# Score units one by one with the products in pieces between them, and an output or value step ahead of the gate step

## The chip, the cores and the metric

One core of a Trainium2 chip (trn2) runs the whole program. The metric is the device time of one execution in microseconds; each kernel was run several times, and medians are given with lowest and highest. The profile's span is about 1.8 us shorter than the time of the same run (461.3 of 463.1). A run is called slow when it is over 1.5% above the fastest of its kernel; such runs are left out of medians and ratios. A run also carries the mean clock that TensorE was granted. That number matters here: in the runs with a trace, 0.995 or 0.996 goes with one stretch of 3.4 us at half clock, 0.999 or 1.00 with none before the last few us.

## The reference

Softmax attention for 8 sequences, 12 heads, 448 tokens, head dimension 64; then a gated feed-forward block on the 3584 x 768 result.

```python
scores = q @ k.transpose(0, 1, 3, 2) / sqrt(64)          # (8, 12, 448, 448)
attn = softmax(scores) @ v                               # (8, 12, 448, 64)
x = attn.transpose(0, 2, 1, 3).reshape(3584, 768)
g = x @ w_gate                                           # (3584, 1536)
out = (g * sigmoid(g) * (x @ w_val)) @ w_out             # (3584, 768)
```

## The kernel before

Work is cut into *pairs* of heads (48), a pair into four *score units* of one key chunk (112 keys): two matmuls of 448 columns into a score buffer, and one exponential of 896 columns on ScalarE. There are three score buffers, and transposed q and k and the gate groups use the same three.

```python
def qk(pr, c):                                    # a score unit
    s = ps_s.tile([128, 2, 512], FP32, tag="s")   # ps_s has 3 buffers
    ...                                           # two matmuls
    nc.scalar.activation(e[:, :, 0:S], s[0:P, :, 0:S], AF.Exp, scale=sm_scale)

def pv(pr):                                       # the product of a pair: 4 x 8 matmuls of 65 columns
    acc = ps_f.tile([128, 512], FP32, tag="f", name="acc")   # ps_f has 2 buffers
    for c in range(NC):
        ...
    nc.vector.reciprocal(...)                     # then one multiply for 6 blocks, two small ones
    ...
```

`copy_v` puts V of a pair beside a column of ones (which gives the sums of the softmax); `turn_x` transposes a pair's result with TensorE into the feed-forward input X. The first six pairs come before any feed-forward work, because X of the first sequence needs all six. That *first batch* is the stage of part 1 of the change:

```python
for pr in range(FIRST):                           # FIRST = 6
    qk_half(pr, 0, ...)                           # two score units
    ...
    if pr in (2, 4):
        for p in range(3):
            copy_v(3 * (pr // 2 - 1) + p)         # VectorE
    elif pr == 3:
        pv(1)                                     # a whole product at once
        turn_x(0)
    ...
    qk_half(pr, 1, turn2)
    if pr == 2:
        pv(0)
    elif pr == 3:
        turn_x(1)
        pv(2)
    ...
```

After that come *visits*: three score units (two in the first four visits), the products of pairs that are due, and some feed-forward steps. A feed-forward step of the first kind (`run_fv`) is a gate group and a value group of 6 matmuls each; of the second kind (`run_o`) an output step of 12 matmuls.

```python
def ffn1_steps(kk, c0, n, hts):
    for fb in range(NFB):
        gp = ps_s.tile([128, 2, 512], FP32, tag="s", name="gp")[:, 0]   # a score buffer
        ...                                       # 6 matmuls
        nc.scalar.activation(sg[:, 0:n], gp[:, 0:n], AF.Tanh, scale=0.5)
        vp = ps_f.tile([128, 512], FP32, tag="f")
        ...                                       # 6 matmuls
        nc.vector.scalar_tensor_tensor(t1[:, 0:n], sg[:, 0:n], 1.0, gp[:, 0:n], ALU.add, ALU.mult)
        nc.vector.scalar_tensor_tensor(hts[:, fb, 0:n], t1[:, 0:n], 0.5 * HS, vp[:, 0:n], ALU.mult, ALU.mult)
```

In 17 visits no product is due. In 12 of these the gate group follows three score units directly and has to wait for a score buffer (below: *bare* visits). The other 5 have only one or two score units, or no gate group, and show no such wait; the flag `bare` in the code holds for all 17.

The softmax here doesn't subtract the row's maximum and nothing guards it: scores larger than these inputs give would overflow.

## Time and profile before

| | before |
|---|---|
| time, median of 3 runs | 463.11 us (463.1 to 464.29) |
| span of the profiled run, mean granted clock | 461.3 us, 0.996 |
| TensorE busy | 442.3 us, 96% |
| gate groups' waits for an exponential | 8.0 us, 12 times |
| first gate group starts at | 34.31 us |
| granted clock in the stretch 15.15 to 18.57 | 0.52 |

The page's first part and its chain of waits say what bounds the kernel; the prediction shows those lines. TensorE's timeline in the kernel before shows how a bare visit looks (start, duration, line, work, number of matmuls; in brackets the idle time just before it and what ended it):

```profile
92.96 0.35 PE L217 MATMUL s<-qkT 64*128 64x448 f16 x2
94.00 1.45 PE L297 MATMUL gp<-X,wg 128*128 128x512 f16 x6 [0.69 <-ACT E L225]
95.29 1.46 PE L309 MATMUL vp<-X,wv 128*128 128x512 f16 x6
```

The last score unit has gone in, and the gate group stands 0.69 us until the first of three exponentials has left its buffer.

### The profile page before, as it was taken

The numbers are of one execution on the slowest core, as the hardware profiler recorded it, in microseconds if no ns is written. First come the engines' busy times: TensorE is split into PE (matmuls) and PEld (weight loads), VectorE is DVE, ScalarE is ACT, GpSimd is POOL, SyncE is SP. The second block draws the span as 40 slices with busy tenths as digits, with TensorE's granted clock in tenths as the row PEclk, the third lists the DMA queues.
The fourth block names the chain that finished last, engine by engine and source line by source line (L and its number), as shares of the span: only waits on it lengthen the run. The fifth ranks groups of instructions, "written<-read, shape, count | busy, mean of one in ns | idle before, by whom it ended". The sixth has DMA issues, their size and how long they took to land.

```text
span 461.3 us, 9838 instructions
## 1 busy us (share of the span) xinstructions
PE 442.3 (96%) x3992; PEld 247.2 (54%) x3992; DVE 207.3 (45%) x480; ACT 237.7 (52%) x350; POOL 137.9 (30%) x222
## 2 busy tenths in 40 slices
PE   7879999999999999999999999999999999999996
PEld 3645566545455656455455565555455556644464
DVE  3576664456553534344344453444435343235400
ACT  6774577655565455635555455654554634222222
POOL 8455607834614225252322404350100000000000
PEclk9899999999999999999999999999999999999999
DMA  9999999999855648894567558973344111210033
GB/s 132 196 200 202 177 193 163 197 171 129 100 84 80 114 93 130 120 110 80 82 114 117 96 98 118 136 97 70 56 67 75 36 21 50 76 34 1 0 104 102
DMA packets 104941, 48.71 MB, mean 106 GB/s; under 512 B 59584, under 2 KB 101440, under 8 KB 104896
## 3 DMA queue, kind: packets, MB, share of 16 engines
q0 software_dynamic: 43296, 23.37, 40.7%
q1 hardware_dynamic: 61504, 24.66, 28.7%
q8 instruction: 31, 0.51, 0.5%
q14 instruction: 14, 0.11, 0.1%
q10 hardware_dynamic: 96, 0.05, 0.0%
HBM read 47.19 MB, written 11.01 MB: 126 GB/s over the span
## 4 chain that ended last, share of the span: by engine, by line
PE 93%; ACT 5%; DVE 1%; issue 0%; ACTq 0%
PE gp L297 24%; PE op L343 24%; PE vp L309 24%; PE acc L242 9%; PE s L217 8%; ACT E L225 4%; PE acc L251 3%; PE wp L107 1%; PE tp L205 1%; ACT osb L350 1%; PE xtp L283 0%; DVE xt L261 0%; DVE xt L268 0%; DVE qkT L191 0%; DVE R L260 0%
## 5 line engine op out<-in xcount | busy, mean ns | idle before, releaser
L225 ACT ACTIVATE E<-s 112x896 f16<-112x896 f32 x192 | 161.7, 920 | 23.1 <-PE s L217 22.9
L297 PE MATMUL gp<-X,wg 128*128 128x384 f16 (+1 forms) x576 | 124.8, 352 | 8.0 <-ACT E L225 8.0
L309 PE MATMUL vp<-X,wv 128*128 128x384 f16 (+1 forms) x576 | 124.6, 352 | 0.0
L343 PE MATMUL op<-wo,hts 128*128 128x384 f16 (+1 forms) x684 | 115.9, 323 | 0.0
L317 DVE SCALAR_TENSOR_TENSOR t<-sg,gp 128x384 f32<-128x384 f32 (+1 forms) x96 | 59.6, 621 | 107.0 <-ACT sg L305 107.0
L305 ACT ACTIVATE sg<-gp 128x384 f32<-128x384 f32 (+1 forms) x96 | 52.7, 549 | 77.5 <-PE gp L297 75.7
L343 PEld LDWEIGHTS <-hts 128*128 128x128 f16 x684 | 66.3, 98 | 44.1 <-issue 0.4
L350 ACT ACTIVATE osb<-op 128x384 f32<-128x384 f32 (+1 forms) x57 | 27.6, 485 | 116.0 <-PE op L343 113.3
L309 PEld LDWEIGHTS <-wv 128*128 128x128 f16 x576 | 56.4, 98 | 52.7
L297 PEld LDWEIGHTS <-wg 128*128 128x128 f16 x576 | 53.1, 97 | 55.6 <-issue 12.4
L165 POOL COPY qk<-q 112x512 f16<-112x512 f16 x37 | 22.9, 620 | 143.5 <-DMA qkT<-qk 142.4
L320 DVE SCALAR_TENSOR_TENSOR hts<-t,vp 128x384 f16<-128x384 f32 (+1 forms) x96 | 59.6, 621 | 10.4 <-DVE t L317 0.5
L242 PEld LDWEIGHTS <-E 112*128 112x128 f16 x1152 | 47.0, 98 | 16.4 <-issue 15.9
L242 PE MATMUL acc<-vo,E 112*128 112x65 f16 x1152 | 52.6, 195 | 0.3 <-DVE X L286 0.3
L217 PE MATMUL s<-qkT 64*128 64x448 f16 x384 | 50.3, 356 | 2.4 <-ACT E L225 1.6
L260 DVE RECIPROCAL R<-acc 128x7 f32<-128x7 f32 x48 | 9.9, 206 | 92.9 <-PE acc L251 92.8
L251 PE MATMUL acc<-vo,E 112*128 112x65 f16 x384 | 43.2, 194 | 0.0
L134 POOL DMA_DIRECT2D vraw<-in_v_dram x40 | 26.6, 666 | 24.0 <-DVE vo L140 9.9
L127 POOL DMA_DIRECT2D k<-in_k_dram x42 | 27.8, 661 | 12.6 <-PE vp L309 8.4
L217 PEld LDWEIGHTS <-qkT 64*128 64x128 f16 x384 | 14.4, 94 | 28.5 <-issue 20.9
L127 POOL DMA_DIRECT2D q<-in_q_dram x42 | 28.0, 667 | 4.1 <-PE tp L205 2.3
L261 DVE TENSOR_TENSOR xt<-acc,R 128x384 f16<-128x384 f32 x48 | 26.8, 558 | 1.7
(38 smaller groups left out, 155.2 us busy)
## 6 DMA issues: line engine op xcount, KB each, us to landing
q<-in_q_dram POOLq DMA_DIRECT2D x37, 112.0 KB, 4.1
k<-in_k_dram POOLq DMA_DIRECT2D x37, 112.0 KB, 4.7
vraw<-in_v_dram POOLq DMA_DIRECT2D x36, 112.0 KB, 4.5
out_dram<-osb SPq DMA_DIRECT2D x7, 336.0 KB, 3.2
wg<-in_moe_w_gate_dram POOLq DMA_DIRECT2D x8, 288.0 KB, 10.9
wv<-in_moe_w_val_dram POOLq DMA_DIRECT2D x8, 288.0 KB, 11.3
wo<-in_moe_w_out_dram POOLq DMA_DIRECT2D x2, 1152.0 KB, 22.7
out_dram<-osb SPq DMA_DIRECT2D x8, 288.0 KB, 3.3
```

The source lines that it names most:

```text
L127: nc.gpsimd.dma_start(dst[:, ds(h0, 2 * n)], flat.rearrange("h (p c) d -> p h (c d)", c=NC))
L217: nc.tensor.matmul(s[:, hx, 0:S], lhsT=t[ts(hx, 64), c * P : c * P + 128], rhs=t[ts(hx, 64), ds(S + (1 - hx) * D, S)], start=True, stop=True,)
L225: nc.scalar.activation(e[:, :, 0:S], s[0:P, :, 0:S], AF.Exp, scale=sm_scale)
L242: nc.tensor.matmul(a7[:, 2 * j + hx], lhsT=e[:, ds(c * EB + 9 * hx + 2 * j, 2)].rearrange("p b x -> p (b x)"), rhs=vo[:, hx, c, 0 : D + 1] ...
L251: nc.tensor.matmul(a7[:, 6], lhsT=e[:, ds(b0, 2)].rearrange("p b x -> p (b x)"), rhs=vo[:, hx, c, 0 : D + 1], start=False, stop=last and h ...
L297: nc.tensor.matmul(gp[:, 0:n], lhsT=wslice("g", fb, cb), rhs=X[kk][:, cb, ds(c0, n)], start=(cb == 0), stop=(cb == NCB - 1),)
L305: nc.scalar.activation(sg[:, 0:n], gp[:, 0:n], AF.Tanh, scale=0.5)
L309: nc.tensor.matmul(vp[:, 0:n], lhsT=wslice("v", fb, cb), rhs=X[kk][:, cb, ds(c0, n)], start=(cb == 0), stop=(cb == NCB - 1),)
L317: nc.vector.scalar_tensor_tensor(t1[:, 0:n], sg[:, 0:n], 1.0, gp[:, 0:n], ALU.add, ALU.mult)
L320: nc.vector.scalar_tensor_tensor(hts[:, fb, 0:n], t1[:, 0:n], 0.5 * HS, vp[:, 0:n], ALU.mult, ALU.mult)
L343: nc.tensor.matmul(op[:, 0:w], lhsT=hts[:, fb, ts(ch, 128)], rhs=wo[oh][:, fb, ds(m0 - oh * OH, w)], start=(fb == 0), stop=(fb == NFB - 1),)
L350: nc.scalar.activation(osb[:, ds(m0, w)], op[:, 0:w], AF.Copy, scale=1.0 / HS)
```

## The change

Part 1 wants the exponentials of the first batch to run without gaps: score units go in one at a time, and from unit 12 up to two *pieces* of a product (8 matmuls, one key chunk) follow each. Single warming matmuls are to keep the clock up, and the first six copies of V move to GpSimd. Part 2 wants the bare visits' wait away: an output step goes first, or, where there is none, the value group before the gate group.

```diff
-NV = 3
+NV = 6
     def copy_v(pr):
-        nc.vector.tensor_copy(Vts[pr % NV][:, :, :, 0:D], vraw[:, pr % VS])
+        eng = nc.gpsimd if pr < FIRST else nc.vector
+        eng.tensor_copy(Vts[pr % NV][:, :, :, 0:D], vraw[:, pr % VS])
@@ the product is cut into pv_chunk(pr, c); turn_x uses 5 matmuls for 4, and in the first batch the product's own accumulator; for 12 pairs one multiply of 448 columns for three @@
@@ the first batch @@
+        for u in range(FIRST * NC):
+            pr, c = divmod(u, NC)
+            qk(pr, c)
 ...
+            elif u >= 6 and c == 2:
+                prep(pr + 2)()
+            if u in (5, 7, 8, 9, 11):
+                dummy(1)
+            if c == 1:
+                if pr in (1, 3):
+                    for p in range(3):
+                        copy_v(3 * (pr // 2) + p)
+                for w in wq.pop(pr, []):
+                    emit(w)
+            if u in (15, 17, 19, 21):
+                turn_x((u - 15) // 2)
+            for _ in range(2):
+                if u >= 12 and pieces[0][0] * NC + pieces[0][1] <= u - 3:
+                    piece()
@@ ffn1_steps @@
+            if val_first[0]:
+                val_first[0] = False
+                vp = ps_f.tile([128, 512], FP32, tag="f", name="vp")
+                group("v", vp)
             gp = ps_s.tile([128, 2, 512], FP32, tag="s", name="gp")[:, 0]
+            group("g", gp)
@@ a visit of the first two sequences' blocks, and of the later ones @@
+            bare = not todo and bool(chunks)
             if adds[max(y for y in adds if y <= x)] < 2:
+                if bare and oq and not fvq:
+                    carry -= run_o()
+                elif bare:
+                    val_first[0] = True
                 carry = run_budget(left() / (end - x) + carry)
             else:
 ...
+                if bare and no:
+                    run_o()
+                    no -= 1
+                elif bare:
+                    val_first[0] = True
```

More of the change, by code (lines that the diff above doesn't have):

```diff
@@ L193, in turn0 @@
                 if t == 0:
-                    nc.vector.tensor_copy(qkT[pr][:, 2 * S :], tp[:, 0, 0:D])
+                    tq = tp
+            nc.vector.tensor_copy(qkT[pr][:, 2 * S :], tq[:, 0, 0:D])
         def turn():
@@ L231, in qk_half, with pv_chunk @@
                 between()
-    def pv(pr):
+    accs = {}
+    def pv_chunk(pr, c):
+        if c == 0:
+            accs[pr] = ps_f.tile([128, 512], FP32, tag="f", name="acc")
         e = Es[pr % NE]
         vo = Vts[pr % NV]
-        acc = ps_f.tile([128, 512], FP32, tag="f", name="acc")
-        a7 = acc[:, 0 : 7 * (D + 1)].rearrange("p (s d) -> p s d", s=7)
-        for c in range(NC):
-            first, last = c == 0, c == NC - 1
-            for j in range(3):
-                for hx in range(2):
-                    nc.tensor.matmul(
-                        a7[:, 2 * j + hx],
-                        lhsT=e[:, ds(c * EB + 9 * hx + 2 * j, 2)].rearrange("p b x -> p (b x)"),
-                        rhs=vo[:, hx, c, 0 : D + 1],
-                        start=first and j + hx == 0,
-                        stop=False,
-                    )
+        a7 = accs[pr][:, 0 : 7 * (D + 1)].rearrange("p (s d) -> p s d", s=7)
+        for j in range(3):
@@ L249, in pv @@
             for hx in range(2):
-                b0 = c * EB + 6 + hx
                 nc.tensor.matmul(
-                    a7[:, 6],
-                    lhsT=e[:, ds(b0, 2)].rearrange("p b x -> p (b x)"),
+                    a7[:, 2 * j + hx],
+                    lhsT=e[:, ds(c * EB + 9 * hx + 2 * j, 2)].rearrange("p b x -> p (b x)"),
                     rhs=vo[:, hx, c, 0 : D + 1],
-                    start=False,
-                    stop=last and hx == 1,
-                )
+                    start=c + j + hx == 0,
@@ L258, in pv @@
+                    stop=False,
+                )
+        for hx in range(2):
+            nc.tensor.matmul(
+                a7[:, 6],
+                lhsT=e[:, ds(c * EB + 6 + hx, 2)].rearrange("p b x -> p (b x)"),
+                rhs=vo[:, hx, c, 0 : D + 1],
+                start=False,
+                stop=c == NC - 1 and hx == 1,
+            )
+        if c < NC - 1:
+            return
         r = attp.tile([128, 8], FP32, tag="R", bufs=2, name="R")
         xt = Xts[pr % NX]
+        n = 7 if pr < XPE else 6
@@ L260, in pv @@
         nc.vector.reciprocal(r[:, 0:7], a7[:, :, D])
         nc.vector.tensor_tensor(
-            xt[:, 0:3].rearrange("p j (h d) -> p (j h) d", h=2),
-            a7[:, 0:6, 0:D],
-            r[:, 0:6].unsqueeze(2).to_broadcast([128, 6, D]),
+            xt[:].rearrange("p j (h d) -> p (j h) d", h=2)[:, 0:n],
+            a7[:, 0:n, 0:D],
+            r[:, 0:n].unsqueeze(2).to_broadcast([128, n, D]),
             ALU.mult,
         )
+        if pr < XPE:
+            return
         for hx in range(2):
@@ L270, in pv @@
             )
+    def pv(pr):
+        for c in range(NC):
+            pv_chunk(pr, c)
     def turn_x(pr):
@@ L279, in turn_x @@
         if pr < XPE:
-            tp = ps_f.tile([128, 512], FP32, tag="f", name="xtp")
-            for j in range(4):
-                n = 128 if j < 3 else D
+            tp = accs[pr] if pr < FIRST else ps_f.tile([128, 512], FP32, tag="f", name="xtp")
+            for j in range(3):
                 nc.tensor.matmul(
-                    tp[:, ds(D + 128 * j if j < 3 else 0, n)], lhsT=xt[:, j], rhs=ident[:, 0:n], start=True, stop=True
+                    tp[:, ds(D + 128 * j, 128)], lhsT=xt[:, j], rhs=ident[:], start=True, stop=True
+                )
+            for hx in range(2):
+                nc.tensor.matmul(
+                    tp[ts(hx, D), 0:D],
+                    lhsT=xt[:, 3, 0:D],
+                    rhs=ident[:, ts(hx, D)],
+                    start=True,
+                    stop=True,
                 )
@@ L291, in turn_x, with group @@
         nc.sync.dma_start_transpose(dst[:, 0:D].rearrange("p (j q) -> p j q", j=1), xt[0:D, 3])
+    val_first = [False]
     def ffn1_steps(kk, c0, n, hts):
         for fb in range(NFB):
-            gp = ps_s.tile([128, 2, 512], FP32, tag="s", name="gp")[:, 0]
-            for cb in range(NCB):
-                nc.tensor.matmul(
-                    gp[:, 0:n],
-                    lhsT=wslice("g", fb, cb),
-                    rhs=X[kk][:, cb, ds(c0, n)],
-                    start=(cb == 0),
-                    stop=(cb == NCB - 1),
-                )
+            gp = vp = None
+            def group(kind, dst):
+                for cb in range(NCB):
+                    nc.tensor.matmul(
+                        dst[:, 0:n],
+                        lhsT=wslice(kind, fb, cb),
+                        rhs=X[kk][:, cb, ds(c0, n)],
+                        start=(cb == 0),
+                        stop=(cb == NCB - 1),
+                    )
+            if val_first[0]:
+                val_first[0] = False
+                vp = ps_f.tile([128, 512], FP32, tag="f", name="vp")
+                group("v", vp)
+            gp = ps_s.tile([128, 2, 512], FP32, tag="s", name="gp")[:, 0]
+            group("g", gp)
             sg = fp.tile([128, 512], FP32, tag="sg")
             nc.scalar.activation(sg[:, 0:n], gp[:, 0:n], AF.Tanh, scale=0.5)
-            yield NCB * n / 2400.0
-            vp = ps_f.tile([128, 512], FP32, tag="f")
-            for cb in range(NCB):
-                nc.tensor.matmul(
-                    vp[:, 0:n],
-                    lhsT=wslice("v", fb, cb),
-                    rhs=X[kk][:, cb, ds(c0, n)],
-                    start=(cb == 0),
-                    stop=(cb == NCB - 1),
-                )
+            if vp is None:
+                vp = ps_f.tile([128, 512], FP32, tag="f", name="vp")
+                group("v", vp)
             t1 = fp.tile([128, 512], FP32, tag="t1")
@@ L322, in ffn1_steps @@
             )
-            yield NCB * n / 2400.0
+            yield
     def ffn2_steps(kk, c0, n, hts, first, last_block):
@@ L381 @@
             nc.vector.memset(e[:, 7::EB], 0.0)
-        for xt in Xts:
-            nc.vector.memset(xt[D:128, 3], 0.0)
         for vo in Vts:
@@ L431, in run_fv @@
             gen, t = fvq.pop(0)
-            for _ in range(2):
-                next(gen)
+            next(gen)
             return 2 * t
@@ L450, in share, with piece @@
             return (at + 1) * total // n - at * total // n
-        for pr in range(FIRST):
-            odd = pr % 2 == 1
-            turn2 = None
-            qk_half(pr, 0, prep(2) if pr == 1 else None)
-            if pr == 0:
+        pieces = [(p, c) for p in range(FIRST) for c in range(NC)]
+        def piece():
+            pv_chunk(*pieces.pop(0))
+        for u in range(FIRST * NC):
+            pr, c = divmod(u, NC)
+            qk(pr, c)
+            if u == 1:
                 dummy(1)
@@ L459 @@
                 dummy(1)
-            if pr > 0:
-                turn2 = prep(pr + 2)
-            if pr in (2, 4):
-                for p in range(3):
-                    copy_v(3 * (pr // 2 - 1) + p)
-            elif pr == 3:
-                pv(1)
-                turn_x(0)
-            elif pr == 5:
-                turn_x(3)
-            for w in wq.pop(pr, []):
-                emit(w)
-            qk_half(pr, 1, turn2)
-            if pr == 0:
-                dummy(2)
-            if pr == 2:
-                pv(0)
-            elif pr == 3:
-                turn_x(1)
-                pv(2)
-            elif pr == 4:
-                turn_x(2)
-                pv(3)
-            elif pr == 5:
-                pv(4)
+            elif u == 3:
+                dummy(2)
+            elif u == 4:
+                prep(2)()
+            elif u >= 6 and c == 2:
[13 more added lines that the diff above has]
+                    piece()
         queue = []
@@ L515 @@
             if x == 0:
+                piece()
                 turn_x(4)
-                pv(5)
+                piece()
+                piece()
                 turn_x(5)
```

## The prediction

> **What bounds the kernel now.** I read the page first, then the waits of TensorE, then the busy time in stretches, then the timelines of TensorE, VectorE, ScalarE and GpSimd up to the first feed-forward block, and last the order of the instructions of both kernels on each engine, which can be listed without a run.
>
> ```profile
> PE 442.3 (96%) x3992; PEld 247.2 (54%) x3992; DVE 207.3 (45%) x480; ACT 237.7 (52%) x350; POOL 137.9 (30%) x222
> PE 93%; ACT 5%; DVE 1%; issue 0%; ACTq 0%
> ```
>
> TensorE is busy for 96% of the span and the chain that ended last runs through it for 93%. Nothing in the change takes matmuls away worth counting, so all that can be won is TensorE's idle or slow time. The waits of TensorE:
>
> ```profile
> PE gp L297 <- ACT E L225: 8.0, 12, 0.7
> PE xtp L283 <- DVE xt L261: 1.7, 3, 0.9
> PE s L217 <- ACT E L225: 1.6, 5, 0.4
> PE tp L205 <- ACT E L225: 1.1, 2, 0.7
> PE s L217 <- DVE qkT L191: 0.6, 1, 0.6
> PE acc L242 <- DVE X L286: 0.3, 1, 0.3
> ```
>
> The first line is 12 gate groups that wait 0.67 us each for an exponential, all after 56 us. The other lines lie in the first 35 us. The stretches there (columns: length, busy time and count of PE, PEld, DVE, ACT, POOL, then granted clock, DMA share, GB/s):
>
> ```profile
> 8.33:11.74 3.41, 2.84 (x40) 1.32 (x39) 1.06 (x4) 3.29 (x5) 3.36 (x5) 1.00 1.17 139
> 11.74:15.15 3.41, 2.09 (x36) 1.24 (x31) 1.07 (x4) 3.41 (x6) 1.53 (x2) 1.00 1.41 189
> 15.15:18.57 3.42, 3.39 (x43) 2.26 (x43) 1.94 (x8) 2.11 (x3) 1.11 (x2) 0.52 1.43 198
> 18.57:21.98 3.41, 3.05 (x70) 2.34 (x68) 2.52 (x7) 2.93 (x4) 2.55 (x4) 0.98 1.32 203
> 21.98:25.39 3.41, 2.49 (x54) 1.75 (x51) 3.24 (x11) 2.22 (x3) 1.56 (x3) 1.00 1.36 198
> ```
>
> ScalarE fills 11.74 to 15.15 completely: 12 exponentials ran there in a row, 10.02 us from 6.72, so 0.835 us each. In the next stretch the clock is 0.52 and ScalarE starves behind two whole product blocks. The first gate matmul starts at 34.31. From 35 us on TensorE's only waits are those 12.
>
> **What the Trainium skill says.** "TensorE: Matmul & The Clock Gate", Part 1, says that a monitor halves the clock for a following window of about 3413 ns after a window with too little activity. The trace agrees: 2.09 us busy of 3.41 was followed by a window at 0.52, 2.49 of 3.41 was not. "PSUM — Partial Sum Buffer", section "Engine vs sequencer instructions", says that ScalarE, VectorE and GpSimd have strict first-in-first-out queues. The trace agrees for GpSimd: its issues wait one behind the other, as below. "SBUF — State Buffer", section "SBUF: two separate sides", says that VectorE (in some modes) and GpSimd hold a shared port for a whole instruction. GpSimd's query load begins at 15.35, after VectorE's copies of V that began at 14.80; that fits, but is one case.
>
> **The change, part 1: the first batch.** It takes the 24 score units one by one, puts up to two pieces of a product (8 matmuls, one key chunk) after each from unit 12, adds single warming matmuls after five units, and moves the six copies of V from VectorE to GpSimd, with six buffers for three. If ScalarE were the bound throughout, exponential 23 would end at 6.72 + 24 x 0.835 = 26.8. After it come: the last piece 0.24 and its drain 0.2, reciprocal 0.21, the multiply, now 448 wide, 0.56 x 448/384 = 0.65, the transposes 0.25, with hand-overs of 0.05: the first group would start near 28.5, against 34.31, 5.8 us sooner. TensorE's own work allows about that: per unit 0.27 for scores, 0.48 for two pieces, and 0.51 for a transposition of q and k every fourth: 10.8 us for units 12 to 23.
>
> But the copies stand in GpSimd's queue, and that is where I expect the loss:
>
> ```profile
> 15.35 0.74 POOL L127 DMA_DIRECT2D q<-in_q_dram  x1 [1.32 <-PE tp L205]
> 18.20 0.71 POOL L127 DMA_DIRECT2D k<-in_k_dram  x1 [2.10 <-PE s L217]
> 18.90 1.64 POOL L151 DMA_DIRECT2D wg<-in_moe_w_gate_dram  x2
> 21.27 0.76 POOL L151 DMA_DIRECT2D wv<-in_moe_w_val_dram  x1 [0.73 <-DMA wg<-in_moe_w_gate_dram]
> 22.71 0.76 POOL L151 DMA_DIRECT2D wv<-in_moe_w_val_dram  x1 [0.67 <-DMA wg<-in_moe_w_gate_dram]
> 24.44 0.74 POOL L127 DMA_DIRECT2D q<-in_q_dram  x1 [0.96 <-DMA wv<-in_moe_w_val_dram]
> ```
>
> The issues recycle eight semaphores, so each waits for an earlier transfer to land, while the DMA is full (198 GB/s). Copies 0 to 2 stand before the load at 15.35 and can run when V lands at 14.80; a GpSimd copy of that shape takes 0.62 (the copies of q and k), so the first is ready at 15.5, when unit 12 needs it. Copies 3 to 5 stand behind the value weight load at 22.71, which waits for gate weights to land. They end at 23.47 + 0.62 = 24.1, 24.7 and 25.3. Unit 18 wants the first of them: 15.2 + 7 x 0.27 + 12 x 0.24 + 2 x 0.51 + 2 x 0.25 = 21.5. So TensorE stands for 2.6 us, and ScalarE, with units up to 18 queued, runs dry at 22.6.
>
> From 24.15, by the order listed: unit 18's pieces 0.48; 19: 0.27 + 0.25 (a turn of x) + 0.48; 20: 0.75; 21: 0.76; 22: 0.27 + 0.51 + 0.24; 23: 0.51; then two scores, pieces 21 to 23 and a turn 1.5. Sum 6.0, end at 30.2; plus 1.5 for the chain above: 31.7. That is 2.6 us won instead of 5.8. If the stall also halves the clock in the window after 25.39 (chunks took 0.44 instead of 0.24 at 0.52), about 1.5 more is lost and 1.1 is won. Weighing the halved clock 0.45, the plain stall 0.35 and no stall (4.8) 0.2, I take 2.2.
>
> **Part 2: visits without products.** Three score units fill the three score buffers, so a gate group after them waits for the first exponential. In nine of the twelve visits an output step of 12 matmuls (1.95 us) now goes first. It needs another pool, whose buffer is long free, and outlasts the 0.67. Nothing else moves: all nine vanish, together 8.0 - (0.63 + 0.69 + 0.63) = 6.05 us.
>
> Four visits put the value group first. In three, and in one early one that had no wait, only one pair of groups is run, so the gate group is now the last thing before the next three scores. The third of those takes the gate group's buffer, which VectorE frees after ScalarE's tanh:
>
> ```profile
> L317 DVE SCALAR_TENSOR_TENSOR t<-sg,gp 128x512 f32<-128x512 f32 x48 | 33.0, 688 | 59.6 <-ACT sg L305 59.6
> L317 DVE SCALAR_TENSOR_TENSOR t<-sg,gp 128x384 f32<-128x384 f32 x48 | 26.6, 554 | 47.5 <-ACT sg L305 47.5
> L305 ACT ACTIVATE sg<-gp 128x512 f32<-128x512 f32 x48 | 28.7, 597 | 49.3 <-PE gp L297 47.6
> L305 ACT ACTIVATE sg<-gp 128x384 f32<-128x384 f32 x48 | 24.0, 500 | 28.2 <-PE gp L297 28.1
> ```
>
> For 512 columns: drain 0.17 + tanh 0.60 + 0.69 + hand-overs 0.13 = 1.59 after the gate group, while the third score is due at 0.1 + 0.48 = 0.58. So a wait of 1.0 replaces one of 0.66: two visits lose 0.4 each, 0.8. For 384 columns the chain is 1.35: the visit at 56.7 us keeps nearly all its loss (won 0.1), because tanh there is held by the three exponentials in both orders; the early visit gets a new wait of 0.75. Before, the value group lay in between and hid this. Six turns of x get a fifth matmul, 0.04 each: 0.2.
>
> Part 2: 6.05 + 0.1 - 0.8 - 0.75 - 0.2 = 4.4 us. VectorE's saving (one wider multiply for three instructions in twelve pairs) is off the path.
>
> **Sum.** 463.1 - 2.2 - 4.4 = 456.5 us, 1.4% faster.
>
> **Rivals.** (A) Everything works as intended: copies on time, no moved waits: 5.8 + 8.0 gives 449 to 450. For it: exponentials have run gaplessly for 12 units. Against it: the queue order above. (B) The waits only move, and the first batch stalls at half clock or worse: 1 + 2.5 gives 459.5 to 460. For it: the single buffer ring of three and the 0.52 stretch. Against it: nine of the twelve visits have the harmless output step. (C) Transfers become the bound as TensorE arrives earlier: the output weights land at about 64.5 and 72.1 (GpSimd's issues that wait for them start at 64.53 and 72.06), the first output group started at 71.8; moved to 68 it still has its half, and the second half is needed some 8 us later. Pair 14's transpose, issued at 73.9, takes 3 to 12 us, needed at 88.2 before. So perhaps a microsecond at most; I leave it out of the sum.
>
> **Range and chances.** First batch 0.5 to 5, part 2 3 to 6: 80% between 453.2 and 460.0. Over 2% needs less than 453.85, which asks that the stall be absent and part 2 whole: 0.17. Slower by 2%: 0.01. Within: 0.82.
>
> **What would show it.** A TensorE wait for GpSimd's copy of V ahead of the first product of pair 3, ending near 24.1; the first value group near 31.7; the granted clock in the window after it; no gate waits for exponentials; new score waits for VectorE's gate product, about 1.0 twice and 0.7 to 0.8 twice. I am wrong if copies 3 to 5 run before 21.5, if a copy takes much more than 0.62, or if output steps first produce waits of their own.

## The result, and the profile after

The changed kernel takes 456.77 us (456.47 to 456.91, 4 runs) beside 463.7 us (463.1 to 464.3, 4 runs) for the kernel before: a ratio of 0.985, 95% interval 0.9831 to 0.9868. A ratio here is the mean time of one kernel's fast runs over that of the other's of the same rounds, so not quite the ratio of the medians. That is 1.5% faster. All four of these runs of the kernel before lie at 463.1 us or above, where its later runs with a halved clock lie (see The experiments); beside its runs without (461.8) the changed kernel is 5.0 us faster, 1.1%.

The page of the changed kernel, its busy line and its chain of waits:

```profile
PE 444.9 (98%) x4009; PEld 247.9 (54%) x4009; DVE 200.2 (44%) x450; ACT 238.7 (52%) x350; POOL 141.7 (31%) x228
...
PE 94%; ACT 3%; DVE 2%; issue 0%; DVEq 0%
```

TensorE is busy for 2.6 us more in a span 6.2 us shorter. The waits of TensorE in the changed kernel (us in total, times, longest):

```profile
PE s L219 <- DVE t L339: 3.1, 4, 0.9
PE wp L107 <- DVE warm L401: 1.2, 1, 1.2
PE acc L293 <- DVE xt L266: 1.0, 1, 1.0
PE acc L245 <- DVE qkT L211: 0.8, 1, 0.8
PE s L219 <- ACT E L227: 0.2, 1, 0.2
```

The 12 gate waits of 8.0 us are gone. In their place four score units wait 3.1 us for VectorE's gate product. The fourth line is a new wait before a product, which I come to below. The stretches of the first batch in the changed kernel, with the columns of the prediction's table:

```profile
11.74:15.15 3.41, 3.05 (x29) 1.38 (x29) 1.18 (x3) 3.41 (x5) 1.53 (x2) 1.00 1.40 185
15.15:18.57 3.42, 3.27 (x64) 2.29 (x63) 1.14 (x5) 3.42 (x5) 3.11 (x6) 1.00 1.43 198
18.57:21.98 3.41, 3.41 (x68) 2.36 (x65) 2.12 (x6) 2.48 (x4) 2.28 (x3) 1.00 1.32 203
21.98:25.39 3.41, 2.65 (x58) 1.95 (x57) 2.06 (x5) 1.73 (x3) 2.75 (x5) 1.00 1.38 199
25.39:28.80 3.41, 3.41 (x72) 2.43 (x71) 2.04 (x4) 2.87 (x4) 2.64 (x4) 1.00 1.35 201
```

The granted clock stays at 1.00. ScalarE is full up to 18.57, and from there it is TensorE that is full (3.41 of 3.41) in two of three stretches, while ScalarE starves. The first feed-forward group, now a value group, starts at 32.89 against 34.31: 1.4 us of the 6.2 come from the first batch (against a run that had the halved stretch), 4.8 from the visits behind it.

The stall before pair 3's first product, on TensorE's timeline in the changed kernel:

```profile
22.43 0.36 PE L219 MATMUL s<-qkT 64*128 64x448 f16 x2
22.73 0.39 PE L207 MATMUL tp<-ident,q 112*64 112x112 f16 x8
22.95 0.36 PE L207 MATMUL tp<-ident,k 112*64 112x112 f16 x8
24.07 0.34 PE L245 MATMUL acc<-vo,E 112*128 112x65 f16 x6 [0.76 <-DVE qkT L211]
```

And GpSimd's timeline there, in the same kernel:

```profile
15.42 1.72 POOL L141 COPY vo<-vraw 112x512 f16<-112x512 f16 x3 [0.79 <-DMA vraw<-in_v_dram]
...
21.18 0.77 POOL L152 DMA_DIRECT2D wv<-in_moe_w_val_dram  x1 [0.69 <-DMA wg<-in_moe_w_gate_dram]
22.64 0.76 POOL L152 DMA_DIRECT2D wv<-in_moe_w_val_dram  x1 [0.69 <-DMA wg<-in_moe_w_gate_dram]
23.39 1.72 POOL L141 COPY vo<-vraw 112x512 f16<-112x512 f16 x3
```

The first of three copies starts at 23.39 and takes about 0.6 us, so it ends near 24.0, just before the product starts at 24.07. The profile names VectorE as the releaser of that wait, but the product doesn't read what VectorE's L211 writes; in three of the experiments below (the third score unit held, value first everywhere, two pairs) the same wait is put down to GpSimd's copy. A releaser is inferred, and where the engine named has no part in the operands, look for one that does.

TensorE's pace, on the same timeline, where nothing waits: one score unit, two pieces (the lines left out are the rest of them), the next score unit:

```profile
25.95 0.36 PE L219 MATMUL s<-qkT 64*128 64x448 f16 x2
26.24 0.35 PE L245 MATMUL acc<-vo,E 112*128 112x65 f16 x6
...
26.83 0.36 PE L219 MATMUL s<-qkT 64*128 64x448 f16 x2
```

Read the starts, not the durations, which overlap: 0.29 us for the scores and 0.59 for the two pieces, 0.88 for a unit; an exponential takes 0.835. The kernel before ran four pieces in a row, then two score units:

```profile
25.45 0.35 PE L242 MATMUL acc<-vo,E 112*128 112x65 f16 x6
25.70 0.34 PE L242 MATMUL acc<-vo,E 112*128 112x65 f16 x6
...
26.51 0.55 PE L217 MATMUL s<-qkT 64*128 64x448 f16 x4
```

A piece with a piece behind it took 0.24 to 0.25 there. The step from the last piece to the scores is 0.1 longer.

The new kind of wait, in a bare visit of the changed kernel:

```profile
95.83 1.47 PE L319 MATMUL vp<-X,wv 128*128 128x512 f16 x6
97.13 1.46 PE L319 MATMUL gp<-X,wg 128*128 128x512 f16 x6
98.52 0.55 PE L219 MATMUL s<-qkT 64*128 64x448 f16 x4
100.00 0.37 PE L219 MATMUL s<-qkT 64*128 64x448 f16 x2 [0.92 <-DVE t L339]
```

Value first, gate second, then the next visit's scores. The first two score units (4 matmuls) find free buffers; the third needs the one that the gate group has just filled, and waits 0.92 us until tanh and the gate product have emptied it.

### The profile page after: what moved, and what is told of

Read it like the earlier page. It is cut to its first block, busy times and chain, and to the rows that moved or that the text cites. A ratio compares the mean times of both kernels' runs of the same rounds, so it can differ in the third digit from the quotient of the medians.

```text
span 455.1 us, 9850 instructions
## 1 busy us (share of the span) xinstructions
PE 444.9 (98%) x4009; PEld 247.9 (54%) x4009; DVE 200.2 (44%) x450; ACT 238.7 (52%) x350; POOL 141.7 (31%) x228
## 4 chain that ended last, share of the span: by engine, by line
PE 94%; ACT 3%; DVE 2%; issue 0%; DVEq 0%
PE op L365 24%; PE gp L319 24%; PE vp L319 24%; PE acc L245 9%; PE s L219 9%; PE acc L253 2%; ACT E L227 2%; PE wp L107 1%; DVE t L339 1%; PE tp L207 1%; ACT sg L334 1%; PE acc L293 0%; DVE xt L266 0%; DVE X L304 0%; PE tp L184 0%
## 5 line engine op out<-in xcount | busy, mean ns | idle before, releaser
L342 DVE SCALAR_TENSOR_TENSOR hts<-t,vp 128x384 f16<-128x384 f32 (+1 forms) x96 | 59.6, 620 | 10.8 <-PE acc L253 0.5
L266 DVE TENSOR_TENSOR xt<-acc,R 128x384 f16<-128x384 f32 (+1 forms) x48 | 27.5, 573 | 1.7
```

Of the source, the lines that this page charges most:

```text
L266: nc.vector.tensor_tensor(xt[:].rearrange("p j (h d) -> p (j h) d", h=2)[:, 0:n], a7[:, 0:n, 0:D], r[:, 0:n].unsqueeze(2).to_broadcast([12 ...
```

## The experiments

Theory at the start: both parts gain; part 1 loses most of its ideal gain to GpSimd's queue, part 2 gives some back to the four waits of score units. Rivals: all of part 1's gain is the clock; the stall is the bound of the first batch; the value-first order is worth having.

In all comparisons the kernel before ran on the same chip as the experiment: 31 runs in all, 461.41 to 464.42. They fall in two heaps: 11 with a mean granted clock of 0.992 to 0.996 (median 463.6) and 20 with 0.998 to 1.00 (median 461.8). Of the profiled ones, that of 0.996 has the stretch at 0.52. So the single stretch of halved clock goes with some 1.8 us and comes and goes between runs of one kernel on one chip. A comparison of a few runs has to heed it. (The changed kernel's own sitting isn't among the 31. It was run at another time.)

### Part 2 alone, on the kernel before

```diff
@@ the kernel before, with val_first in ffn1_steps and in the visits as in the change; the first batch untouched @@
+            bare = not todo and bool(chunks)
+                if bare and oq and not fvq:
+                    carry -= run_o()
+                elif bare:
+                    val_first[0] = True
```

> The kernel before with only the order of the feed-forward steps of the change. My theory (the two parts add up, and part 2 is worth what the traces show, 6.2 us of span less the 1.4 us by which the first group came sooner): 4.8 us less than before, first gate or value group near 34.3 us as before, 12 gate waits for exponentials gone, four score waits for VectorE of 0.6 to 0.9. Rival (part 2 gains only because TensorE arrives earlier from part 1, or the parts overlap): less than 4 us.

Measured: 458.21 us (457.33 to 459.49, 6 runs), ratio 0.9912 (0.9891 to 0.9932). Its profiled run has the halved stretch (0.50) as that of the kernel before has, so the two spans compare directly: 461.3 to 456.4, **4.9 us**. Its waits have the 3.2 us of score units in place of the 8.0 of gate groups:

```profile
PE s L217 <- DVE t L321: 3.2, 4, 0.9
```

8.0 less 3.2 is 4.8: the wait table accounts for the whole gain of part 2.

### Part 1 alone

```diff
-            bare = not todo and bool(chunks)
+            bare = False
```

> The changed kernel with the old order of feed-forward steps. My theory: 1.4 us less than before (first group near 32.9 us), less some 0.2 for the wider turns of x later on, with the 12 gate waits of 8.0 us all back. Rival (parts overlap): 2 us or more less than before.

Measured: 461.79 us (461.59 to 461.97, 5 fast runs, all with clock 0.999 or 1.0), ratio 0.9984 (0.9966 to 1.0002). The gate waits are back (8.0 us, 12 times). Against the profiled run of the kernel before, which had the halved stretch, the span is 1.1 us shorter (460.2 for 461.3). Against the 20 runs of before without it (461.8) it is no shorter at all. So part 1 does not speed up the program; what it wins is that none of these five runs paid for a halved stretch. The sixth run, the slow one at 469.98 us with clock 0.982, has no trace; it may have paid for a longer one (see Two pairs of groups in such visits). And part 2 on top of it, from this kernel to the changed one, is 461.79 to 456.77, 5.0 us, which agrees with the first experiment.

### Output steps first, without the value-first order

```diff
-                    val_first[0] = True
+                    pass
```
(at both places)

> The changed kernel with output steps first where they were, but no value group first anywhere. My theory (the value-first order moves the wait to the third score of the next visit and makes it longer): gate waits return in three visits, 0.6 to 0.7 each, the four score waits (3.1 us in all) go, so about 1.2 us faster than the changed kernel. Rival (value first wins what it removes, 1.9 us): about 2 us slower than the changed kernel.

Measured: 455.40 us at the median of five fast runs (four at 455.24 to 455.55, and one at 459.88 with clock 0.989; one slow run is left out), ratio 0.9866 (0.9832 to 0.99). The waits of TensorE:

```profile
PE gp L319 <- ACT E L227: 2.0, 3, 0.7
```

Three gate groups wait 2.0 us in all, and no score unit waits for a gate product. So with this half of part 2 the kernel is 1.4 us slower than without it, by medians of two sittings; 3.1 less 2.0 us of waits, read from the traces, accounts for 1.1 of that. (The ratios to the kernel before, 0.9866 here and 0.985, don't show it: the run at 459.88 is in the mean.)

### The warming matmuls alone, on the kernel before

```diff
-            qk_half(pr, 0, prep(2) if pr == 1 else None)
+            qk_half(pr, 0, prep(2) if pr == 1 else (lambda: dummy(1)) if pr == 2 else None)
+            if pr in (1, 2):
+                dummy(1)
 ...
             qk_half(pr, 1, turn2)
+            if pr in (1, 2):
+                dummy(1)
```

> The kernel before with nothing but the five warming matmuls of the change, at the same units. Theory W (the first batch gained because the clock no longer falls to 0.52 at 15 us): granted clock 1.00 there, first gate group 1.2 to 1.6 us sooner, the whole gain of part 1. Theory P (the pieces between single scores gained it): clock may rise, but the first gate group moves by less than 0.5 us, because the next waits take the place.

Measured: 463.01 us (461.55 to 463.45, 6 runs), ratio 1.0002 (0.998 to 1.0024); two of the six runs still have clock 0.996. The profiled run has 1.00 where the kernel before has 0.52, but its first gate group starts at 34.22, hardly sooner than 34.31: this run's start was late, with ScalarE idle for about 1 us before 10 us. The theory that a little warming is all that part 1 needs is not borne out; the scatter hides anything under a microsecond.

### The change without its warming matmuls

```diff
-            if u in (5, 7, 8, 9, 11):
-                dummy(1)
```

> The changed kernel without its five warming matmuls. Theory W (they keep the clock up): some runs or all show a stretch at about 0.5 between 15 and 19 us and are 1 to 1.5 us slower, mean clock 0.996; runs scatter as those of the kernel before did (clock 0.996 or 1.0). Rival (pieces and scores alone keep it up, the warming only costs 5 x 0.21 us of TensorE): the same or up to 0.5 us faster, clock 1.0 in all runs.

Measured: 456.67 us (456.36 to 457.0, 4 runs), ratio 0.9872 (0.9848 to 0.9896): the same as the changed kernel. Two of the four runs have the halved stretch and are at 457.0 and 456.6, the two others at 456.36 and 456.73. The profiled one, in stretches:

```profile
11.74:15.15 3.41, 1.96 (x26) 1.09 (x23) 1.21 (x4) 3.41 (x5) 1.55 (x3) 1.00 1.37 178
15.15:18.57 3.42, 3.29 (x38) 2.12 (x38) 0.27 (x2) 2.82 (x4) 2.83 (x5) 0.53 1.42 198
18.57:21.98 3.41, 3.41 (x75) 2.52 (x73) 2.64 (x6) 2.22 (x3) 2.52 (x4) 0.97 1.32 202
21.98:25.39 3.41, 3.41 (x68) 2.35 (x64) 2.21 (x6) 2.54 (x4) 2.75 (x5) 1.00 1.38 202
```

The clock is halved for a window, and still the first value group starts at 32.97, against 32.89 with warming. The stall is missing from the waits of this run: TensorE came later to pair 3, when V's copy was ready. That fits a reading in which the time lost to the clock would otherwise have been spent standing before pair 3, so that warming gains nothing while the stall is behind it; no run has warming and stall both taken away.

### All six copies of V early

```diff
-                if pr in (1, 3):
-                    for p in range(3):
-                        copy_v(3 * (pr // 2) + p)
+                if pr == 1:
+                    for p in range(6):
+                        copy_v(p)
```

> The changed kernel with all six copies of V behind the first one in GpSimd's queue, ahead of the weight loads of the second slice. My prediction's theory: the wait before the first product of pair 3 (0.76 us, ending at 24.1) goes, and the first group comes that much sooner: 0.5 to 0.8 us faster; not more, because TensorE's own work from unit 12 on fills the time. Rival 1 (the stall governs what follows, 2.6 us as predicted): over 1.5 us faster. Rival 2 (the wait was for VectorE's transposition copy, as the profile names it): no change, the wait stays.

Measured: 456.49 us (456.16 to 457.84, 5 runs), ratio 0.9875 (0.9852 to 0.9898). The wait before pair 3 is gone, which shows that it was GpSimd's queue (the first six copies now run from 15.71 to 19.1, ahead of the weight loads). The first value group starts at 32.37, 0.52 us sooner; the medians differ by 0.28, which is inside the scatter. TensorE's stretches in this run:

```profile
18.57:21.98 3.41, 3.41 (x69) 2.35 (x64) 2.35 (x6) 2.47 (x4) 3.41 (x5) 1.00 1.32 202
21.98:25.39 3.41, 3.41 (x77) 2.62 (x75) 2.53 (x6) 2.54 (x3) 2.27 (x4) 1.00 1.37 200
25.39:28.80 3.41, 3.41 (x65) 2.23 (x61) 2.10 (x5) 2.83 (x4) 2.14 (x3) 1.00 1.35 200
```

Three full stretches on end, at clock 1.00, while ScalarE is busy 2.47 to 2.83 of 3.41. With the stall taken away, TensorE's own matmuls bound the first batch from 18.57 on, not the exponentials, for which the batch was cut up.

### The copies of V on VectorE

```diff
-        eng = nc.gpsimd if pr < FIRST else nc.vector
+        eng = nc.vector
```

> The changed kernel with the six copies of V on VectorE again, six buffers kept. If GpSimd's queue order made the wait: the wait before pair 3 goes, 0.4 to 0.8 us faster, the first copy ready sooner (0.23 us each instead of 0.62). If VectorE's own queue becomes the wait (its transposition copies and multiplies of 0.62 us stand before): a VectorE wait of similar size, no change or slower.

Measured: 460.78 us (460.24 to 461.51, 6 runs, clock 0.991 to 0.996 in all), ratio 0.9966 (0.9948 to 0.9984): 4.0 us slower than the changed kernel. VectorE's timeline:

```profile
12.30 0.18 DVE L211 COPY qkT<-tp 128x64 f16<-128x64 f16 x1
14.80 0.70 DVE L141 COPY vo<-vraw 112x512 f16<-112x512 f16 x3 [2.32 <-DMA vraw<-in_v_dram]
15.41 0.61 DVE L208 COPY qkT<-tp 128x896 f16<-128x896 f16 x1
15.94 0.18 DVE L211 COPY qkT<-tp 128x64 f16<-128x64 f16 x1
```

The copies wait 2.32 us for V to land, and behind them in the queue stands the copy of pair 3's transposed q and k (L208), without which no further score unit can start: TensorE waits 1.1 us for it at 16.18, and ScalarE runs out of work. Both stretches from 15.15 to 21.98 then have a clock of 0.75. So part 1 needs the copies off VectorE, at least where they stand in this order, though they take longer on GpSimd (three in 1.72 us, against three in 0.70).

### The third score unit behind the feed-forward groups

On top of the kernel without value-first: in the three bare visits where only one pair of groups runs, two score units go first, then gate and value group, then the third score unit.

```diff
-            for pr, c in chunks:
+            first = adds[max(y for y in adds if y <= x)] < 2
+            hold = not todo and len(chunks) == 3 and first and bool(fvq)
+            for pr, c in chunks[:2] if hold else chunks:
                 qk(pr, c)
 ...
                 carry = run_budget(left() / (end - x) + carry)
+                if hold:
+                    qk(*chunks[2])
```

> The changed kernel with no value group first, and in the three visits without products and without an output step the third score unit behind the gate and value groups, so that the gate group takes the third score buffer, which is free. My theory: neither the gate waits (2.0 us without value first) nor the score waits (3.1 us with it): 3.1 us faster than the changed kernel, some 453.7 us, over 1.9% faster than before. Rival (the next visit's scores then wait for exponentials, since ScalarE gets the third unit late): less than 2 us.

Measured: 455.56 us (455.29 to 455.91, 4 runs), ratio 0.9851 (0.983 to 0.9871): no better than the kernel without value-first (455.40). The waits:

```profile
PE s L219 <- ACT E L227: 1.9, 4, 0.7
PE acc L245 <- POOL vo L141: 1.4, 2, 1.1
```

The gate groups no longer wait, but the held score unit and the next visit's three make four in a row over three buffers, and the fourth waits for the first exponential, 0.4 us in the visit at 56 us and up to 0.7 in the others. The rival was right: the wait has moved, not gone. (The second line is the copy of V again, with its right name.)

### Value first in all twelve bare visits

```diff
-                if bare and no:
-                    run_o()
-                    no -= 1
-                elif bare:
+                if bare:
                     val_first[0] = True
```

> The changed kernel with the value group first also in the nine later visits that have an output step, which stays at their end. My theory (value first is harmless where something as long as tanh and VectorE's product stands between the gate group and the third score of the next visit): no gate waits, the same four score waits of 3.1 us, the same time as the changed kernel within 0.3 us. Rival (value first costs by itself, 0.25 us or more more per visit): some 2 us slower, new waits in the nine visits.

Measured: 457.72 us (456.62 to 457.86, 6 runs), ratio 0.9887 (0.9863 to 0.991). No new kind of wait: the same four score waits, 3.1 us. The nine visits that now take the value group first end with an output step, which gives VectorE its time. The median is 0.95 above the changed kernel's, where at most 0.3 was expected; of this the later first value group of the profiled run (33.27 for 32.89) explains 0.4; the rest I leave open. So no wait comes from the value-first order as such, but from a gate group as the *last* work before three scores.

### Two pairs of groups in such visits

If that is so, a second pair behind the first, in the order value, gate, gate, value, should take both waits away. What it takes from the budget of its visit is carried over, so later visits run less.

```diff
-                carry = run_budget(left() / (end - x) + carry)
+                budget = left() / (end - x) + carry
+                for _ in range(min(len(fvq), 2 if bare else 1)):
+                    budget -= run_fv()
+                carry = run_budget(budget)
```

> The changed kernel with two pairs of groups in each visit without products and without output step (value, gate, gate, value), and at least one in the others. Theory: both the gate wait and the score wait go, since a group stands on either side of the gate groups and TensorE's 4.6 to 5.9 us are longer than ScalarE's 3.0 to 3.7: all 3.1 us of score waits gone, 453.6 us. Rival (waits move once more, to the value buffers or to ScalarE in visits that now hold one pair): less than 1.5 us.

Measured: 453.31 us (452.14 to 457.58, 6 runs), ratio 0.9789 (0.9761 to 0.9818). No gate group and no score unit waits for the other any more. Five runs lie at 452.14 to 453.67 with clock 0.999 or 1.0. The sixth, which is the profiled one, took 457.58 with clock 0.987. Its waits and stretches:

```profile
PE acc L245 <- POOL vo L141: 1.5, 1, 1.5
```

```profile
21.98:25.39 3.41, 1.89 (x44) 1.58 (x41) 1.84 (x5) 1.23 (x2) 2.74 (x5) 0.87 1.38 199
25.39:28.80 3.41, 3.41 (x42) 2.20 (x40) 1.45 (x3) 1.37 (x2) 2.78 (x5) 0.50 1.34 201
28.80:32.20 3.40, 3.40 (x42) 2.06 (x39) 0.62 (x1) 2.09 (x3) 1.93 (x3) 0.50 1.33 201
```

The stall for V's copy was 1.5 us here (0.8 in the changed kernel), only 1.89 of 3.41 us of that stretch were busy, and for the next two the clock is at 0.50. By the clock record of the trace the half clock lasted from 24.5 to 34.8 us, three windows of 3.41 us, though TensorE had work nearly all the time; in the other traces it lasted one, and no run shows why. The first value group starts at 37.41, 4.5 us later than in the changed kernel. This is the halved clock after the stall to which the prediction gave 0.45, and it costs 4.5 us where 1.5 was said. The interval of the ratio reaches over 0.98, so the verdict at 2% is "unclear".

How often does it happen? Of the 32 runs of kernels with this first batch (the changed kernel and five experiments: part 1 alone, no value first, third score unit held, value first everywhere, two pairs), four have a clock of 0.982 to 0.989 and are 4.5 to 8.2 us longer than the others of their kernel: this one, 459.88 and 463.05 without value first, and 469.98 with part 1 alone. The two that are called slow are among them. None of the kernel before's 31 runs has a clock under 0.992, and none of the 16 runs of the three kernels that copy V earlier on GpSimd has one under 0.999. That fits the stall as the trigger, but only this one run has a trace, so it is not shown.

### V earlier and the products from unit 9

V of the first three pairs is loaded before q and k of pairs 4 and 5, the copies stand earlier in GpSimd's queue, and the pieces begin three units sooner.

```diff
-        load_qk16(4)
         load_v(0, GP)
+        load_qk16(4)
         load_v(3, GP)
 ...
-                if u >= 12 and pieces[0]...
+                if u >= 9 and pieces[0]...
```
(and the copies of V moved, ahead of and behind the first value weight load; the transposition of pair 4's q and k from unit 10 to 13, three turns of x two units earlier, and two warming matmuls left out)

> The changed kernel with the first three V loaded ahead of the queries and keys of pairs 4 and 5, their copies ahead of the first value weight load, the next three behind it, products from unit 9 on and two warming matmuls fewer. Theory (between units 12 and 23 TensorE is full, between 6 and 11 it is not): the first group starts 1.0 to 2.0 us sooner than 32.9, and no wait for a copy of V; 455 us. Rival (ScalarE or the transfers are the bound of the batch): under 0.5 us, with new waits for V, for q and k of pair 4, or idle TensorE.

Measured: 457.53 us (456.9 to 457.82, 6 runs), ratio 0.9887 (0.9864 to 0.991), and the first value group at 33.81, 0.9 us later. The wait before pair 3 is gone, but there are new ones: two for VectorE, and one for V's copy before the very first product (14.14):

```profile
PE acc L245 <- DVE X L304: 1.8, 2, 0.9
...
PE acc L245 <- POOL vo L141: 0.9, 1, 0.9
```

A product's accumulator is one of two buffers, and in the first batch the turn of x now uses the same accumulator again; a product that comes early finds it not yet copied out by VectorE (L304), twice 0.9 us. The rival was right: an earlier start of the products is stopped by the two accumulators and by V itself.

### Two pairs and early copies together

> This is the combination of the two edits that went the right way: at least one pair of value and gate groups in every visit and two in the visits without products and without output steps (which measured 453.3 us alone), and the six copies of V early in GpSimd's queue (which took the wait before pair 3 away and brought the first value group 0.52 us sooner). Theory: the two lie in different stretches and add, but the second is worth little, since TensorE's own work bounds the first batch: 452.6 to 453.3 us, no gate waits, no score waits for the gate product, no wait of a product for GpSimd's copy of V, first value group near 32.4, and no stretch of halved clock between 22 and 32 us as the profiled run of the two-pairs kernel had, because the stall that brought it on is gone; so its runs should scatter less than that kernel's (452.1 to 457.6). Rival: the halved clock of that run had nothing to do with the stall: then some runs here too are at 456 to 458. Second rival: the early copies collide with the copies of VectorE or the loads, and the time is above 454.

Both edits above, on the changed kernel. Measured: **452.51 us** (452.21 to 453.87, 5 runs, all with clock 0.999 or 1.0), ratio 0.9792 (0.9769 to 0.9815). All the waits of TensorE of 0.2 us and more that are left:

```profile
PE wp L107 <- DVE warm L401: 1.2, 1, 1.2
PE acc L293 <- DVE xt L266: 1.0, 1, 1.0
PE s L219 <- ACT E L227: 0.2, 1, 0.2
```

The span is 450.8 us and TensorE is busy for 444.2 of it, 99%. The first value group starts at 32.09. Beside the two-pair kernel's five undisturbed runs (median 453.0) that is 0.5 us at most; their ranges overlap. None of five runs had the halved clock that one of six had there. That fits the reason given (no stall, no halving), but five runs cannot show it. It is the fastest kernel, 0.9% faster than the change as given; the interval of its ratio reaches from 0.977 to 0.9815, so "over 2% faster than before" is likely but not certain.

## Why the prediction was right or wrong

The time was right to 0.3 us (456.5 predicted, 456.77 measured), but that is partly luck: two of its terms were off in opposite directions, the first batch by about 1 us and the visits by 0.5, and the 463.1 us from which it was reckoned came from a run with a halved stretch.

**What bounds the kernel: right.** Waits and slow clock were all that could be won. The span fell by 6.2 us, and the waits of TensorE in the visits account for 4.9 of it (8.0 less 3.1).

**The first batch, 2.2 us predicted: too much.** Spans with a comparable second part give 1.1 (before to part 1 alone) and 1.3 (part 2 alone to the changed kernel), and both compare with a run that had the halved stretch. Against runs of the kernel before without it, part 1 is worth nothing (461.79 against 461.8). The prediction took that stretch, which the profile before showed, for a property of the kernel. It is one of about every third run. The step that failed was the pace of TensorE, "per unit 0.27 for scores, 0.48 for two pieces". A score unit between pieces took 0.29 and two pieces 0.59, and a turn of x 0.42 where 0.25 was said. The durations fit groups of their kind in a row: four pieces in a row last 1.06 from the first to the scores behind them (the lines shown above), four times 0.24 and a step of 0.1. The gain of cutting the work fine is paid for with such a step at each change of kind. What the step consists of, no run shows. From unit 12 to the end of unit 23 TensorE took 14.0 us (15.69 to 29.70), of which 0.8 is the stall and 1.7 are four turns of x that the prediction's 10.8 had left out. The rest is 11.5. The prediction's own terms add up to 10.5, not 10.8 (12 x 0.75 and three transpositions of 0.51), and to 9.8 for the work that was done, since three of the last units had one piece only: the pace cost 1.7 us more than set down. At 0.88 us for a unit with two pieces TensorE is slower than the 0.835 of an exponential before any turn or transposition is added. So the exponentials could not run gaplessly, whatever the queue did: the "5.8 us sooner" was never to be had.

**The loss to GpSimd's queue: right in place and time, wrong in size.** The wait before pair 3 ended at 24.07, predicted 24.1, by the chain of waits that was named; moving the copies ahead of the weight loads took it away. But TensorE reached it at 23.3, not at 21.5, for the reason above, and the stall was 0.8 instead of 2.6. The late arrival by itself cost nothing, since the copy set the end of the wait. The work after it took 7.3 (24.07 to 31.35) instead of 6.0, again the mis-sized pace: the sum put the first group at 31.7, and it started at 32.89. The chain behind the last piece was 1.54 for 1.5. The halved clock after the stall, given 0.45, was in none of the changed kernel's four runs and in four of the 32 with the same first batch. The weighing itself was off too: 0.45 x 1.1, 0.35 x 2.6 and 0.2 x 4.8 make 2.4, not 2.2.

**The visits, 4.4 us predicted: too little, by 0.5.** Measured 4.9 and 5.0. All nine output-first visits lost their wait, without new ones: right. The value group goes first in six visits, not four; the two that were missed, at 32.89 and 38.0 us, get no wait. The others got the waits named, 0.92 twice where 1.0 was said, 0.68 where 0.75 was, and the one at 56.7 us kept its loss, 0.61 for 0.63. The waits that the two of 512 columns replace were 0.69 and 0.63, so these visits lost 0.23 and 0.29 where 0.4 each was set down: 0.3 of the 0.5. The other 0.2 is the charge for the fifth matmul of a turn. Both measured gains compare kernels with the same turns, so they cannot show it, and no run isolates it.

**The rivals.** (A), all as intended at 449 to 450, fails at the first batch by TensorE's pace. Only the last kernel, which goes beyond the change, comes within 3 us of it. (B), the waits only move, holds for the three visits with value first that had a wait before, and for none of the nine others. (C), transfers, showed in no wait of TensorE after 35 us. (One of its readings is doubtful: of the two issues that are said to wait for the output weights, the profile puts the first, at 64.53, down to TensorE.)

**What the change as given left.** Its value-first rule lost 1.4 us to leaving the gate step as it was (456.77 against 455.40, of which the waits show 1.1). Two pairs in these visits are 3.5 us faster than the changed kernel (453.31), and 2.1 faster than the one without value-first.

## What to carry to other kernels

When a wait is to be filled with other work, ask what is then the last thing before the next use of the same buffers: a step moved ahead of the waiting one also moves the waiting one next to its successor, and only enough work behind it hides its drain. When cutting matmul groups finer to feed another engine, take the pace from groups that already alternate, and compare it with that engine's own pace before hoping for its bound. And before winning back a stretch of halved clock that one profile shows, see in how many runs it is there; and look at the clock of the runs that are left out as slow.

## What the Trainium skill lacked or had wrong

- "TensorE: Matmul & The Clock Gate", "HAM oscillation — how this bites in real kernels", gives the rule as no idle gaps of TensorE over about 3.4 us; no section of the page gives the busy share that a window needs. Here no gap was near that long, and the share told the two cases apart. Laid along the clock changes in each trace, the 3.41 us just before a half clock held 1.93 (without warming), 1.98 (two pairs), 2.06 (before), 2.09 (part 2 alone) and 2.16 us (copies on VectorE) of TensorE's busy time, 57% to 63%. The least busy windows at full clock, up to 36 us, that no half clock followed held 2.16 (value first everywhere, 22.25 to 25.66) and 2.31 us (third score unit held, 21.75 to 25.16). So in these traces the boundary lies near 2.2 of 3.41 us. In the changed kernel's trace every stretch of 3.41 us that starts between 5 and 33 us holds 2.45 us or more. In that of the kernel before some do and some don't, by where the window starts.
- Part 1 of that page says that the clock is either full or half and that the window is free-running. That agrees: 0.50 in the records (15.3 to 18.7 in the kernel before), the stretches at 0.75 with copies on VectorE are one half window (16.9 to 20.3) lying across two of them, and that 11 of 31 runs of one kernel had it and 20 had not fits a phase that differs from run to run.
- The same page, "Back-to-back issue gap", puts a stream of weight loads and matmuls at about 81 ns for 128 columns and 131 ns for 512. Here six gate matmuls of 512 columns with a new weight load each took 1.30 us (95.83 to 97.13), 216 ns each, and eight of 65 columns 0.24 us, 30 ns each. Both are what an estimate by the page's formula for an isolated matmul gives (columns / 2.4 + 2.5 ns: 216 and 30), not its sustained figures. No page has the step between groups of different shape: about 0.1 us a change here (a score unit between pieces took 0.29, three in a row 0.68, four pieces and the step behind them 1.06).
- "GPSIMD Engine Reference", "4.1 Engine selection", calls one-input work on GpSimd roughly line-rate and gives a factor against VectorE for two-input work alone. It doesn't say what a one-input 16-bit copy costs beside VectorE: one of 112 x 512 elements took 0.57 us there (three in 1.72) and 0.23 on VectorE (three in 0.70), 2.5 times as long; spans on GpSimd are rough, but the products' start agrees with them.
- No page read says that in a profile a wait can be put down to an engine whose output the waiting instruction doesn't read (0.76 us put down to VectorE here, 1.10, 1.25 and 1.52 us to GpSimd's copy in three other runs).
